# Where the passes of w_in's conversion and the multiplies of h's steps stand in the engines' orders

## The chip, the core and the metric

The kernel runs on one core of a Trainium2 chip. Five queues work at the same time and meet only through semaphores: TensorE (PE in the profile; its weight loads are PEld), VectorE (DVE), ScalarE (ACT), GpSimd (POOL) and the DMA queue of SyncE (SP). Each carries out its own instructions in the order in which the program issues them. The metric is the time of one execution in microseconds (us); lower is better.

## The reference: what is computed

Windowed attention over 4 x 576 tokens with 8 heads, then two feed-forward stages, all in fp32 with tolerances that TensorE's fast fp32 format alone doesn't meet:

```python
scores = scale * np.matmul(q, k.transpose(0, 1, 3, 2))     # window of 64, masked
attn = softmax(scores)                                     # exp(s - max) / (sum + 1e-9)
x = matmul(attn, v)                                        # 2304 x 512
h1 = ((x @ w1) * (x @ w2)) @ w3                            # 512 -> 1024
x2 = h1 @ w_out                                            # 1024 -> 512
h = x2 @ w_in                                              # 512 -> 2048
g = h * (1.0 / (1.0 + np.exp(-h)))
out = g @ w_out2                                           # 2048 -> 512
```

The weights arrive as 64-bit floats. The kernel reads them as pairs of 32-bit words and turns them into fp32 itself.

## The kernel before, in words

**Numbers.** A value that goes into TensorE is split in a high part (a cast on ACT) and a low part (value less high part, on DVE or POOL); a product takes three matmuls, high by high, high by low, low by high.

**Conversion of a weight chunk** of 128 x 512 takes these passes: `scale` (ACT, from the high words), `rest` (ACT, from the low words), `fraction` (a shift on DVE), `sign` (an and-or of two SBUF tensors on DVE, after it an add on POOL). `Chunk` (from line 92) does so for weights that are split at once (`high_part` on ACT at line 145, `low_part` at line 149). `Stored` (line 153) does it for w_in and stores the fp32 words in DRAM (`w_in32`), from where the later stage loads them (`r_load`).

**First part, blocks 0 to 5** (`phase_a`, 384 tokens each). A block has 24 units on PE: 16 units of 12 matmuls for x@w1 and x@w2 (`ab`, line 561; the odd ones end in `a`, the multiply of line 569 on DVE, and p's split: an ACT cast and a POOL subtract, lines 81 and 84), then 8 units of 12 matmuls for x2 (`x`, line 581). Before each unit one half of an attention group is issued (`half`): the even half has the scores on PE, the scores' minima on DVE (line 319), the value matmuls (`o`), the transposes of the group before (`t`, line 352), p-transposed's casts on ACT and its subtracts on DVE (lines 362 to 367), and the exponentials on ACT (line 330). The odd half has the normalising on DVE (a reduce, a reciprocal and the multiply of line 342, whose result `sm` the next transposes read), the sums of the values (lines 394 to 398) and the preparation of a later group's q, k and v (lines 284 to 291). So a group is two units, and a block takes 12 groups. Attention ends in block 4.

**w_in's conversion** runs beside blocks 1 to 4. It has 16 chunks. A list `trickle` holds their pieces in order, and `drop` runs one piece per unit, as the first thing behind the half: two loads first, then for each chunk `scale`, `rest`, `fraction`, `sign`, `store` and the load of the chunk after next. That is one chunk in 6 units, or 3 groups.

**Second part.** In the last seven units of block 5, and then in slots s = 1 to 23 of seven steps k = 0 to 6, h is made in seven products of Strassen's kind per slot (`product`, line 743, six matmuls each) into two PSUM tiles: `hx` for k = 0, 2, 4 and `hy` for k = 1, 3, 5, 6. A product that begins a tile afresh (k = 0, 1, 4, 5) has to wait until the tile's last reader is done. `read` adds the pieces up on DVE (line 638, as all of `add` and `sub`) and has ACT take the sigmoid; `multiply` (DVE) makes g, `divide` splits it (ACT cast, POOL subtract), and `out_tile` multiplies it with w_out2 (line 797, six matmuls, k = 0 to 5). `background` does, in each step, the conversion of w_out2's chunks (`convert_to`, slots 1 to 7), the preparation of the next slot's w_in pieces (`jit_part`, tables `JIT_AT` and, in block 5, `J5`) and of the next x operand (slots 5 to 8). The order in a step is product, read, background, multiply, divide, out_tile.

Of the kernel before, what the change touches and what calls it, by code (L numbers as in the profile page):

```python
# [42 lines left out]
def tile_window_attention_ffn(ctx, tc, qkv, vp, mask, ident, w1, w2, w3t, w_out, w_in, w_out2, out):  # L43
# [109 lines left out]
    class Stored(Chunk):  # L153
# [3 lines left out]
        def pieces(self):  # L157
# [16 lines left out]
            def sign():  # L174
                nc.vector.scalar_tensor_tensor(
                    out=self.b, in0=self.high, scalar=-0x80000000, in1=self.b, op0=ALU.bitwise_and, op1=ALU.bitwise_or
                )
                nc.gpsimd.tensor_tensor(out=self.b, in0=self.b, in1=self.r, op=ALU.add)
# [4 lines left out]
            return [self.load, scale, rest, fraction, sign, store]  # L183

    weights = {}
    line = []
    done = {"load": 0, "step": 0}
# [214 lines left out]
    def half(h):  # L402
# [4 lines left out]
        if not odd:  # L407
            if g < NG:
                scores(g)
            if 2 <= g <= NG + 1:  # L410
                sums.append(values(g - 2))
                if plain(g - 2):
                    sums.pop()()
# [129 lines left out]
    def phase_a(blk, hooks):  # L543
# [9 lines left out]
        for s in range(16):  # L553
# [11 lines left out]
            if m == 0:  # L565
                a_sb = slot(f"a{blk}_{f}", "st", [2, NB], bufs=4)
                nc.scalar.copy(out=a_sb[:, 0], in_=acc)
            else:
                nc.vector.tensor_tensor(out=a_sb[:, 1], in0=acc, in1=a_sb[:, 0], op=ALU.mult)
                split(p[f][:, 0], p[f][:, 1], a_sb[:, 1], "act", "pool")  # L570
        for o in range(4):
            acc = accumulator(f"x2_{blk}_{o}", [128, NB])
            for f in range(8):
# [6 lines left out]
                for n, (l, r) in enumerate(PASSES):  # L580
# [3 lines left out]
                    )  # L584
            x2 = slot(f"x2s{blk}_{o}", "st", [NB], bufs=4)
# [13 lines left out]
    with tc.manual_schedule():  # L599
# [5 lines left out]
        trickle = []  # L605
        for i in range(16):
# [3 lines left out]
            trickle.append(c.pieces())  # L610
        for a, b in zip(trickle, trickle[2:] + [()] * 2):
            a.extend(b[:1])
        trickle = trickle[0][:1] + trickle[1][:1] + [f for p in trickle for f in p[1:]]

        def drop(n):
            if trickle:
                trickle.pop(0)()

        for blk in range(1, NBLK - 1):
            phase_a(blk, drop)  # L620
        while trickle:
            drop(0)
# [25 lines left out]
        for f in (0, 1, 2, 3, 4, None, None, None, 5, 8, 6, 7, 9, 10, 11, 12, 13, 14, 15):  # L648
# [3 lines left out]
            tag = f"w{f if f < 8 else f + 8}"  # L652
# [30 lines left out]
        def jit_part(s, part):  # L683
# [13 lines left out]
            elif part == 1:  # L697
                sub(nc.vector, a[:, 1], one, f32(a[:, 0]))
                sub(nc.vector, d[:, 1], a22, f32(d[:, 0]))
# [15 lines left out]
        JIT_AT = {0: (2,), 1: (3, 0), 2: (1,), 3: (4,), 4: (5,), 5: (6,)}  # L715
# [46 lines left out]
        def read(s, k):  # L762
# [3 lines left out]
            one, two, three = tmp["v"]  # L766
# [9 lines left out]
            elif k == 4:  # L776
                add(nc.vector, three, x, one)
                finished(s, k, three)
# [80 lines left out]
        def background(s, k):  # L859
# [11 lines left out]
            if 1 <= s < PAIRS and done["step"] < len(line):  # L871
                n = BLOCK_STEPS + 2 * (s - 1) + (k >= 2) + (k >= 5)
                if s < 3:
                    n = BLOCK_STEPS + 3 * (s - 1) + k // 2
                else:
                    n += 2
                convert_to(n)
                loads_to(begin + min(n + 2, 10 if s == 1 else NLINE))
# [9 lines left out]
        def step(s, k):  # L888
            if s < NSLOT:
# [3 lines left out]
                read(s, k)  # L893
            background(s, k)
            multiply()
            divide()
# [7 lines left out]
        J5 = {8: (0, 0), 9: (0, 1), 10: (0, 2), 11: (0, 3), 12: (0, 4), 13: (0, 5), 14: (0, 6)}  # L904
        J5 |= {18: (1, 0), 19: (1, 1), 20: (1, 2), 21: (1, 3), 22: (1, 4), 23: (1, 5)}

        def hooks5(n):
# [14 lines left out]
            if n == 17:  # L922
                t = slot("tmp", "xb", [4, NB])
                tmp["v"] = [t[:, i] for i in range(3)]
                tmp["sg"] = [t[:, 3], xe[:, 2304 - NB : 2304]]
            if n == 16:
                raw[1] = slot("r_w5", "w5", [4, 256])
# [7 lines left out]
            if n >= 8:  # L935
                loads_to(begin + (4 if n < 16 else 5))
            if n in X5:
                X5[n][0](*X5[n][1:])
            if n in J5:
                jit_part(*J5[n])  # L940
# [89 lines left out]
```

## Time and profile before

| | us |
|---|---|
| median of 3 runs | 876.49 (876.15 to 876.94) |
| the profiled execution | 877.07 |
| its span | 875.3 |
| PE busy | 831.3 |
| DVE, ACT, POOL busy | 621.6, 560.8, 533.4 |

The span runs from the first to the last instruction of the program. Busy times are sums over one engine's instructions; matmuls are pipelined, so their busy time is more than what they hold the engine for. The granted clock is full in all slices. A column "idle before" names the engine's pause ahead of an instruction and what ended it.

### The profile page before, as it was taken

How to read it: one execution, taken by the hardware profiler on the slowest of the kernel's cores; microseconds unless marked ns; L12 is line 12 of the kernel's file. 1: busy time of each engine (PE TensorE's matmuls, PEld its weight loads, DVE VectorE, ACT ScalarE, POOL GpSimd, SP SyncE). 2: the span in 40 equal slices, each digit the busy share in tenths (PEclk: the TensorE clock that was granted, in tenths of full speed). 3: DMA queues.
4: the chain of work that ended last, by engine and by line, in shares of the span. 5: the costliest groups of instructions: out<-in, count | busy, mean ns of one | idle time of the engine just before them, and what ended most of it. 6: DMA issues, size and time to landing. Idle time of an engine off the chain costs nothing.

```text
span 875.3 us, 14089 instructions
## 1 busy us (share of the span) xinstructions
PE 831.3 (95%) x4410; PEld 744.7 (85%) x4410; DVE 621.6 (71%) x1404; ACT 560.8 (64%) x1389; POOL 533.4 (61%) x588
## 2 busy tenths in 40 slices
PE   5999999999998998999999999999999999999998
PEld 2455899988998998998999977878889898898896
DVE  5889867688778777877548588878745558655544
ACT  5889778878887788778646465545634345544333
POOL 4768676667666766766656576675644556545341
PEclk9999999999999999999999999999999999999999
DMA  8998234434544544444252451211210300301001
GB/s 289 320 315 275 78 96 128 143 120 148 167 124 128 166 142 126 155 136 132 65 190 91 136 195 49 97 34 39 97 49 25 114 32 25 120 25 34 16 1 72
DMA packets 57130, 102.66 MB, mean 117 GB/s; under 512 B 5472, under 2 KB 34912, under 8 KB 57056
## 3 DMA queue, kind: packets, MB, share of 16 engines
q1 hardware_dynamic: 53600, 97.05, 34.1%
q10 hardware_dynamic: 3456, 4.72, 1.5%
q8 instruction: 35, 0.57, 0.3%
q14 instruction: 39, 0.32, 0.1%
HBM read 88.11 MB, written 13.63 MB: 116 GB/s over the span
## 4 chain that ended last, share of the span: by engine, by line
PE 49%; DVE 17%; ACT 12%; issue 8%; POOL 2%; ACTq 0%; DVEq 0%; POOLq 0%
PE o L797 18%; PE hy L743 9%; PE hx L743 7%; PE ab L561 7%; PE x L581 5%; ACT sm L330 3%; DVE j L638 2%; DVE qkhi L291 1%; DVE sm L342 1%; ACT pt L364 1%; DVE ot L397 1%; DVE sm L319 1%; DVE hl L149 1%; DVE tmp L638 1%; ACT qkhi L284 1%
## 5 line engine op out<-in xcount | busy, mean ns | idle before, releaser
L797 PE MATMUL o<-hl,gp 128*128 128x512 f32 x504 | 133.3, 394 | 0.0
L743 PE MATMUL hy<-xop,j 128*128 128x384 f32 x576 | 116.3, 336 | 4.0 <-DVE tmp L638 4.0
L561 PE MATMUL ab<-xa,hl 128*128 128x384 f32 x576 | 119.0, 341 | 0.0
L561 PE MATMUL ab<-xb,hl 128*128 128x384 f32 x576 | 115.4, 334 | 0.0
L743 PEld LDWEIGHTS hy<-xop,j 128*128 128x128 f32 x576 | 102.5, 188 | 14.2 <-DVE tmp L638 6.4
L797 PEld LDWEIGHTS o<-hl,gp 128*128 128x128 f32 x504 | 93.1, 188 | 13.1
L638 DVE TENSOR_TENSOR tmp<-hy,tmp 128x384 f32<-128x384 f32 x96 | 53.2, 555 | 67.7 <-PE hy L743 38.4
L561 PEld LDWEIGHTS ab<-xb,hl 128*128 128x128 f32 x576 | 101.2, 188 | 0.0
L561 PEld LDWEIGHTS ab<-xa,hl 128*128 128x128 f32 x576 | 99.1, 188 | 0.0
L743 PE MATMUL hx<-xop,j 128*128 128x384 f32 x432 | 87.7, 337 | 4.3 <-DVE tmp L638 3.0
L398 POOL TENSOR_TENSOR xr<-ot 128x128 f32<-128x128 f32 x55 | 33.2, 604 | 93.5 <-DVE ot L397 88.3
L797 PE MATMUL o<-hl,gq 128*128 128x512 f32 x324 | 85.9, 393 | 0.0
L743 PEld LDWEIGHTS hx<-xop,j 128*128 128x128 f32 x432 | 76.0, 188 | 11.3 <-DVE tmp L638 5.2
L288 POOL TENSOR_TENSOR klo<-qk,qkhi 64x192 fp32r<-64x192 f32 x110 | 73.3, 667 | 7.6 <-ACT qkhi L284 2.7
L797 PEld LDWEIGHTS o<-hl,gq 128*128 128x128 f32 x324 | 60.3, 188 | 11.2
L330 ACT ACTIVATE sm<-sm,nm 128x192 f32<-128x192 f32 x144 | 64.5, 450 | 7.0 <-DVE nm L319 5.7
L581 PE MATMUL x<-p,wp 128*128 128x384 f32 x360 | 68.6, 339 | 0.0
L759 ACT ACTIVATE xe<-tmp 128x384 f32<-128x384 f32 x48 | 25.2, 525 | 67.4 <-DVE tmp L638 67.1
L137 POOL TENSOR_TENSOR cv_b<-cv_b,cv_r 128x512 int32<-128x512 int32 x32 | 47.9, 1498 | 25.4 <-DVE cv_b L133 15.7
L581 PEld LDWEIGHTS x<-p,wp 128*128 128x128 f32 x360 | 61.8, 188 | 0.0
L638 DVE TENSOR_TENSOR tmp<-hx,tmp 128x384 f32<-128x384 f32 x48 | 26.7, 555 | 49.1 <-PE hx L743 34.5
L84 POOL TENSOR_TENSOR gp<-tmp,gp 128x384 fp32r<-128x384 f32 x34 | 38.0, 1116 | 35.3 <-ACT gp L81 35.3
(145 smaller groups left out, 1923.9 us busy)
## 6 DMA issues: line engine op xcount, KB each, us to landing
qk<-in_qkv SPq DMA_DIRECT2D x55, 384.0 KB, 3.2
words<-in_w_out SPq DMA_DIRECT2D x24, 512.0 KB, 5.4
r<-w_in SPq DMA_DIRECT2D x22, 512.0 KB, 3.4
words<-in_w3t SPq DMA_DIRECT2D x16, 512.0 KB, 6.0
words<-in_w SPq DMA_DIRECT2D x16, 512.0 KB, 6.5
xe<-in_w_in SPq DMA_DIRECT2D x16, 512.0 KB, 4.5
v<-in_qkv SPq DMA_DIRECT2D x55, 96.0 KB, 2.7
x2d<-x2s ACTq DMA_DIRECT2D x24, 192.0 KB, 1.9
```

The source lines that it names most:

```text
L84: (nc.vector if eng_lo == "dve" else nc.gpsimd).tensor_tensor(out=lo, in0=src, in1=f32(hi), op=ALU.subtract)
L137: nc.gpsimd.tensor_tensor(out=x, in0=b, in1=self.r, op=ALU.add)
L149: eng.tensor_tensor(out=self.parts[:, 1], in0=f32(self.b), in1=f32(self.parts[:, 0]), op=ALU.subtract)
L288: nc.gpsimd.tensor_tensor(out=k_lo[g % 2][hs, h * 192 : h * 192 + 192], in0=t[hs, n], in1=f32(hi[hs, n]), op=ALU.subtract)
L330: nc.scalar.activation(out=x, in_=x, func=AF.Exp, scale=-1.0, bias=nm[:, h : h + 1], accum_out=sums_of[g % 2][:, h, 0:1])
L398: nc.gpsimd.tensor_tensor(out=xr[:, c, r : r + 128], in0=t[:, 0:128], in1=t[:, 128:256], op=ALU.add)
L561: nc.tensor.matmul(acc, lhsT=w[:, l, fs], rhs=x[k // 2][:, k % 2, r, :], start=(k == 0 and n == 0), stop=(k == 3 and n == 2),)
L581: nc.tensor.matmul(acc, lhsT=wp[f][:, l, o * 128 : (o + 1) * 128], rhs=p[f][:, r, :], start=(f == 0 and n == 0), stop=(f == 7 and n == 2),)
L638: eng.tensor_tensor(out=out, in0=a, in1=b, op=op)
L743: nc.tensor.matmul(bank[name], lhsT=w[:, l, at + kt], rhs=x[:, kt, r, :], start=(fresh and kt == 0 and n == 0), stop=(kt == 1 and n == 2), ...
L759: nc.scalar.activation(out=sg, in_=src, func=AF.Sigmoid)
L797: nc.tensor.matmul(oacc[t], lhsT=g[:, l, cols], rhs=weights["out", 2 * p + i][:, r, :], start=(p == 0 and i == 0 and n == 0), stop=(p == P ...
```

## The change

It changes five things.

1. w_in's passes no longer run first in a unit. A dictionary `between` holds them by unit, and `squeeze` runs them at three places: DVE's passes in an even half behind the scores' minima, ahead of p-transposed's subtracts; ACT's passes in an odd unit ahead of p's cast, or ahead of x2's copy.
2. `sign` is cut in two halves of 256 columns, in two even units; the POOL add is issued with the second. A chunk is spread over more units (scale in unit 6i+1, rest 6i+3, fraction 6i+4, the signs 6i+6 and 6i+8, the store 6i+10, the load of chunk i+1 in 6i+2). Signs and store of the last chunk are issued behind block 4.
3. In h's steps the multiply of k = 2 runs ahead of the background, that of k = 6 in the next slot's step 0, ahead of that step's background; those of k = 4 and 5 stay behind it.
4. The sum of k = 4 is written over hx in PSUM, in place of a third temporary; sigmoid and multiply read it there. The two results `sg` lie in one tile, and raw[1] lies in `xr`.
5. w_out2's conversion: chunk 5 moves into block 5, and slots 1 and 2 get fewer passes; the second conversion of a slot stands in k = 3 in place of 5. The subtract of piece d gets a step of its own (part 7), and the casts of part 0 and the subtract of part 1 come one step earlier.

```diff
@@ -171,19 +171,27 @@
-            def sign():
+            def sign(i):
+                n = slice(i * 256, i * 256 + 256)
                 nc.vector.scalar_tensor_tensor(
-                    out=self.b, in0=self.high, scalar=-0x80000000, in1=self.b, op0=ALU.bitwise_and, op1=ALU.bitwise_or
+                    out=self.b[:, n], in0=self.high[:, n], scalar=-0x80000000, in1=self.b[:, n],
+                    op0=ALU.bitwise_and, op1=ALU.bitwise_or,
                 )
-                nc.gpsimd.tensor_tensor(out=self.b, in0=self.b, in1=self.r, op=ALU.add)
+                if i:
+                    nc.gpsimd.tensor_tensor(out=self.b, in0=self.b, in1=self.r, op=ALU.add)
...
-            return [self.load, scale, rest, fraction, sign, store]
+            return [self.load, scale, rest, fraction, lambda: sign(0), lambda: sign(1), store]
...
+    between, unit_of = {}, [0]
+
+    def squeeze(u):
+        if u in between:
+            between.pop(u)()
...
@@ -407,6 +415,7 @@
             if g < NG:
                 scores(g)
+            squeeze(unit_of[0])
...
@@ -567,6 +576,7 @@
                 nc.vector.tensor_tensor(out=a_sb[:, 1], in0=acc, in1=a_sb[:, 0], op=ALU.mult)
+                squeeze(unit_of[0] - 1)
                 split(p[f][:, 0], p[f][:, 1], a_sb[:, 1], "act", "pool")
...
@@ -582,6 +592,7 @@
+            squeeze(unit_of[0] - 1)
             x2 = slot(f"x2s{blk}_{o}", "st", [NB], bufs=4)
...
@@ -602,24 +613,32 @@
-            trickle.append(c.pieces())
-        for a, b in zip(trickle, trickle[2:] + [()] * 2):
-            a.extend(b[:1])
-        trickle = trickle[0][:1] + trickle[1][:1] + [f for p in trickle for f in p[1:]]
+            load, scale, rest, fraction, sign0, sign1, store = c.pieces()
+            at = 6 * i
+            chunks.append((load, store))
+            between[at + 1], between[at + 3] = scale, rest
+            between[at + 4], between[at + 6], between[at + 8] = fraction, sign0, sign1
 
         def drop(n):
-            if trickle:
-                trickle.pop(0)()
-
+            u = unit_of[0]
+            if u % 6 == 2 and 0 < u // 6 < 15:
+                chunks[u // 6 + 1][0]()
+            if u >= 10 and (u - 10) % 6 == 0:
+                chunks[(u - 10) // 6][1]()
+            unit_of[0] += 1
...
@@ -645,11 +664,11 @@
-        for f in (0, 1, 2, 3, 4, None, None, None, 5, 8, 6, 7, 9, 10, 11, 12, 13, 14, 15):
+        for f in (0, 1, 2, 3, 4, 5, None, None, None, 6, 7, 8, 9, 10, 11, 12, 13, 14, 15):
...
-            tag = f"w{f if f < 8 else f + 8}"
+            tag = f"w{f if f < 6 else f + 10 if f < 14 else f - 8}"
...
@@ -696,6 +715,7 @@
                 sub(nc.vector, a[:, 1], one, f32(a[:, 0]))
+            elif part == 7:
                 sub(nc.vector, d[:, 1], a22, f32(d[:, 0]))
...
-        JIT_AT = {0: (2,), 1: (3, 0), 2: (1,), 3: (4,), 4: (5,), 5: (6,)}
+        JIT_AT = {0: (2, 0), 1: (3, 1), 2: (7,), 3: (4,), 4: (5,), 5: (6,)}
...
             elif k == 4:
-                add(nc.vector, three, x, one)
-                finished(s, k, three)
+                add(nc.vector, x, x, one)
+                finished(s, k, x)
...
@@ -869,13 +889,9 @@
-                n = BLOCK_STEPS + 2 * (s - 1) + (k >= 2) + (k >= 5)
-                if s < 3:
-                    n = BLOCK_STEPS + 3 * (s - 1) + k // 2
-                else:
-                    n += 2
+                n = BLOCK_STEPS + 2 * (s - 1) + 1 + (k >= 3) + (s > 1 or k >= 6)
                 convert_to(n)
-                loads_to(begin + min(n + 2, 10 if s == 1 else NLINE))
+                loads_to(begin + min(n + 2, NLINE))
...
@@ -891,9 +907,15 @@
                 product(s, k)
                 read(s, k)
+            if k in (0, 2):
+                multiply()
+            if k == 0:
+                divide()
             background(s, k)
-            multiply()
-            divide()
+            if 2 < k < 6:
+                multiply()
+            if k < 6:
+                divide()
...
-                tmp["v"] = [t[:, i] for i in range(3)]
-                tmp["sg"] = [t[:, 3], xe[:, 2304 - NB : 2304]]
+                tmp["v"] = [t[:, i] for i in range(2)]
+                tmp["sg"] = [t[:, i] for i in (2, 3)]
...
-                raw[1] = slot("r_w5", "w5", [4, 256])
+                raw[1] = slot("r_xr", "xr", [4, 256])
```

DVE in blocks 1 to 4, between two multiplies `a` of line 569 (578 after the change). Names: pt is p-transposed, rs and sm the sums and the weights of attention, ot the sums of the values, cv_b the converted words, xe the raw ones. Before:

```order
L365 TENSOR_TENSOR pt_978<-t_3952,pt_978 128x2x128
L367 TENSOR_TENSOR pt_976<-t_3952,pt_976 64x64 x2
L172 TENSOR_SCALAR cv_b<-cv_b 128x512
L338 TENSOR_REDUCE rs_3945<-es_82 128x2
L340 RECIPROCAL rs_3945<-rs_3945 128x2
L342 TENSOR_TENSOR sm_73<-sm_73,rs_3945 128x384
L396 TENSOR_TENSOR ot_3983<-o_3948,ot_3983 64x256
L397 TENSOR_TENSOR ot_3983<-o_3948,ot_3983 64x256
L291 TENSOR_TENSOR qkhi_3989<-qk_3839,qkhi_3989 64x256
L175 SCALAR_TENSOR_TENSOR cv_b<-xe,cv_b 128x512
L569 TENSOR_TENSOR a_2_3978<-ab_5_4003,a_2_3978 128x384
```

And now:

```order
L327 ISA nm_3951 128x1
L172 TENSOR_SCALAR cv_b<-cv_b 128x512
L373 TENSOR_TENSOR pt_978<-t_3960,pt_978 128x2x128
L375 TENSOR_TENSOR pt_976<-t_3960,pt_976 64x64 x2
L346 TENSOR_REDUCE rs_3952<-es_82 128x2
L348 RECIPROCAL rs_3952<-rs_3952 128x2
L350 TENSOR_TENSOR sm_73<-sm_73,rs_3952 128x384
L404 TENSOR_TENSOR ot_3991<-o_3956,ot_3991 64x256
L405 TENSOR_TENSOR ot_3991<-o_3956,ot_3991 64x256
L299 TENSOR_TENSOR qkhi_3997<-qk_3844,qkhi_3997 64x256
L578 TENSOR_TENSOR a_2_3986<-ab_5_4009,a_2_3986 128x384
```

The fraction stood between the subtracts of pt and the normalising, the sign ahead of the multiply a. The fraction now stands behind the minima (line 327), and each half of the sign stands at that same place in the next two groups (line 176).

POOL in the same blocks; klo, vhl and p are low parts, xr the sums of the values, L178 (181) the add of the conversion. Before:

```order
L398 TENSOR_TENSOR xr<-ot_3983 128x128
L288 TENSOR_TENSOR klo_75<-qk_3839,qkhi_3989 64x192 x2
L84 TENSOR_TENSOR vhl_3994<-v_3761,vhl_3994 128x3x64
L178 TENSOR_TENSOR cv_b<-cv_b,cv_r 128x512
L84 TENSOR_TENSOR p_3780<-a_2_3978,p_3780 128x384
```

And now:

```order
L296 TENSOR_TENSOR klo_75<-qk_3685,qkhi_3836 64x192 x2
L84 TENSOR_TENSOR vhl_3841<-v_3607,vhl_3841 128x3x64
L84 TENSOR_TENSOR p_3785<-a_0_3825,p_3785 128x384
L181 TENSOR_TENSOR cv_b<-cv_b,cv_r 128x512
L406 TENSOR_TENSOR xr<-ot_3911 128x128
```

The add stood ahead of p's subtract; now it stands behind it and ahead of the next sums of values.

DVE in a slot of h's steps that has two conversions (lines 130, 133, 149); hx and hy are the products, j the next slot's weights, tmp and xe the sums and g. Before, from k = 1 to k = 4:

```order
L638 TENSOR_TENSOR tmp<-hy_1_6635,tmp 128x384
L130 TENSOR_SCALAR cv_b<-cv_b 128x512
L133 SCALAR_TENSOR_TENSOR cv_b<-words,cv_b 128x512
L149 TENSOR_TENSOR hl<-cv_b,hl 128x512
L638 TENSOR_TENSOR j_0_6002<-r_6178,j_0_6002 128x512
L638 TENSOR_TENSOR j_3_6005<-r_6178,j_3_6005 128x256
L638 TENSOR_TENSOR tmp<-hx_0_6618,tmp 128x384
L638 TENSOR_TENSOR tmp<-hy_1_6635,tmp 128x384
L638 TENSOR_TENSOR tmp<-hx_4_6697,tmp 128x384
```

And now:

```order
L657 TENSOR_TENSOR tmp<-hy_1_6654,tmp 128x384
L657 TENSOR_TENSOR j_0_6020<-r_6204,j_0_6020 128x512
L657 TENSOR_TENSOR tmp<-hx_0_6620,tmp 128x384
L657 TENSOR_TENSOR j_3_6023<-r_6204,j_3_6023 128x256
L657 TENSOR_TENSOR tmp<-hy_1_6654,tmp 128x384
L130 TENSOR_SCALAR cv_b<-cv_b 128x512
L133 SCALAR_TENSOR_TENSOR cv_b<-words,cv_b 128x512
L149 TENSOR_TENSOR hl<-cv_b,hl 128x512
L657 TENSOR_TENSOR hx_4_6714<-hx_4_6714,tmp 128x384
```

The multiply of k = 2 (tmp<-hx_0) had five subtracts and passes ahead of it behind the sum of k = 1, now one; the conversion comes behind the sum of k = 3.

## Rows read from the trace of the kernel before

**Rows 1.** The waits of PE, longest in total: us, times, longest.

```profile
PE t L352 <- DVE sm L342: 17.8, 20, 1.7
```

**Rows 2.** The chain in order of time, end of block 0: start, length, what.

```profile
139.50 4.17 PE x L581 x24
...
160.51 4.17 PE ab L561 x24
```

**Rows 3.** Windows, blocks 1 to 3, then 4: length; busy PE, PEld, DVE, ACT, POOL.

```profile
160.27:368.08 207.81, 193.35 (x1191) 189.18 (x1190) 163.39 (x515) 168.48 (x493) 140.35 (x192) 1.00 0.47 145
368.08:434.29 66.21, 61.96 (x381) 60.91 (x380) 49.63 (x153) 51.05 (x149) 43.42 (x58) 1.00 0.33 106
```

**Rows 4.** Windows: slots 1 to 7 of h's steps together, then slot 8.

```profile
492.54:613.52 120.98, 112.83 (x547) 97.34 (x547) 99.21 (x132) 65.13 (x129) 78.97 (x69) 1.00 0.27 93
613.52:629.16 15.64, 15.64 (x79) 14.05 (x79) 13.17 (x17) 11.05 (x22) 9.73 (x9) 1.00 0.23 85
```

**Rows 5.** Timeline, two groups of block 2: start, us, engine, line, what, idle before.

```profile
243.67 0.90 DVE L172 TENSOR_SCALAR cv_b<-cv_b 128x512 int32<-128x512 int32 x1
...
245.58 0.52 PE L352 MATMUL t<-id_sb,sm 128*128 128x128 f32 x3 [0.72 <-DVE sm L342]
...
246.68 0.84 DVE L175 SCALAR_TENSOR_TENSOR cv_b<-xe,cv_b 128x512 int32<-128x512 int32 x1
...
249.29 1.30 POOL L178 TENSOR_TENSOR cv_b<-cv_b,cv_r 128x512 int32<-128x512 int32 x1
...
249.30 0.42 DVE L365 TENSOR_TENSOR pt<-t,pt 128x256 fp32r<-128x256 f32 x1 [0.64 <-ACT pt L364]
...
250.54 1.00 POOL L84 TENSOR_TENSOR p<-a,p 128x384 fp32r<-128x384 f32 x1
...
250.71 1.25 DVE L342 TENSOR_TENSOR sm<-sm,rs 128x384 f32<-128x384 f32 x1
...
252.10 0.52 PE L352 MATMUL t<-id_sb,sm 128*128 128x128 f32 x3 [1.08 <-DVE sm L342]
```

**Rows 6.** Timeline, one group of block 0, where no conversion of w_in runs.

```profile
133.78 0.56 DVE L569 TENSOR_TENSOR a<-ab,a 128x384 f32<-128x384 f32 x1
...
134.37 0.51 ACT L81 CAST q<-a 128x384 fp32r<-128x384 f32 x1 [0.83 <-DVE a L569]
...
136.93 0.56 DVE L342 TENSOR_TENSOR sm<-sm,rs 128x384 f32<-128x384 f32 x1
...
139.01 0.49 PE L352 MATMUL t<-id_sb,sm 128*128 128x128 f32 x3
139.12 0.56 DVE L569 TENSOR_TENSOR a<-ab,a 128x384 f32<-128x384 f32 x1
```

**Rows 7.** Groups of instructions by line: ACT's scale; busy us, mean ns | idle before.

```profile
L164 ACT ACTIVATE cv_b<-xe 128x512 f32<-128x512 f32 x16 | 10.4, 652 | 0.0
```

**Rows 8.** Timeline, slot 4 and the start of slot 5.

```profile
554.42 0.79 PE L743 MATMUL hx<-xop,j 128*128 128x384 f32 x3 [0.66 <-DVE tmp L638]
...
560.28 1.67 POOL L137 TENSOR_TENSOR cv_b<-cv_b,cv_r 128x512 int32<-128x512 int32 x1 [1.09 <-DVE cv_b L133]
...
560.72 1.78 DVE L638 TENSOR_TENSOR j<-sums,j 128x512 fp32r<-128x512 f32 x1
...
563.49 1.31 PE L743 MATMUL hy<-xop,j 128*128 128x384 f32 x6 [0.46 <-DVE tmp L638]
564.09 0.94 DVE L638 TENSOR_TENSOR xe<-tmp,xe 128x384 f32<-128x384 f32 x1 [0.65 <-ACT xe L759]
```

**Rows 9.** Instructions on the tile tmp: count, then min/median/max ns.

```profile
L638 DVE TENSOR_TENSOR tmp<-hx,tmp x48: 543/558/559, 477.7 to 858.5; 128x384 f32<-128x384 f32 x48
...
L638 DVE TENSOR_TENSOR xe<-tmp,xe x48: 544/558/1659, 484.5 to 864.6; 128x384 f32<-128x384 f32 x48
```

**Rows 10.** Timeline, block 2, among its units of x2.

```profile
285.20 1.30 POOL L178 TENSOR_TENSOR cv_b<-cv_b,cv_r 128x512 int32<-128x512 int32 x1
...
285.27 1.64 DVE L342 TENSOR_TENSOR sm<-sm,rs 128x384 f32<-128x384 f32 x1
```

More of the change, by code (lines that the diff above doesn't have):

```diff
@@ L604, in tile_window_attention_ffn @@
         phase_a(0, lambda n: steps_to(W12_B + 24 + (n + 1) * (20 - W12_B) // 6, (nc.vector, nc.gpsimd)))
-        trickle = []
+        chunks = []
         for i in range(16):
@@ L609, in tile_window_attention_ffn @@
             c = Stored(None, w_in[k * 128 : (k + 1) * 128, cols], xe[:, i % 2 * 1024 : i % 2 * 1024 + 1024], w_in32[k, :, cols])
-            trickle.append(c.pieces())
-        for a, b in zip(trickle, trickle[2:] + [()] * 2):
-            a.extend(b[:1])
-        trickle = trickle[0][:1] + trickle[1][:1] + [f for p in trickle for f in p[1:]]
-        def drop(n):
-            if trickle:
-                trickle.pop(0)()
+            load, scale, rest, fraction, sign0, sign1, store = c.pieces()
[3 more added lines that the diff above has]
+            between[at + 4], between[at + 6], between[at + 8] = fraction, sign0, sign1
+        def drop(n):
+            u = unit_of[0]
[4 more added lines that the diff above has]
+            unit_of[0] += 1
+        chunks[0][0]()
+        chunks[1][0]()
         for blk in range(1, NBLK - 1):
             phase_a(blk, drop)
-        while trickle:
-            drop(0)
+        for u in sorted(between):
+            between.pop(u)()
+        chunks[15][1]()
         late.close()
@@ L762, in read @@
         def read(s, k):
-            one, two, three = tmp["v"]
+            one, two = tmp["v"]
             x, y = bank["hx"], bank.get("hy")
@@ L903, in tile_window_attention_ffn @@
         X5 |= {10: (x_sum, 3), 11: (x_op, 0, 3), 13: (x_op, 0, 4), 14: (x_op, 0, 5), 16: (x_op, 0, 6)}
-        J5 = {8: (0, 0), 9: (0, 1), 10: (0, 2), 11: (0, 3), 12: (0, 4), 13: (0, 5), 14: (0, 6)}
-        J5 |= {18: (1, 0), 19: (1, 1), 20: (1, 2), 21: (1, 3), 22: (1, 4), 23: (1, 5)}
+        J5 = {8: (0, 0), 9: (0, 1), 10: (0, 7, 2), 11: (0, 3), 12: (0, 4), 13: (0, 5), 14: (0, 6)}
+        J5 |= {18: (1, 0), 19: (1, 1), 20: (1, 7, 2), 21: (1, 3), 22: (1, 4), 23: (1, 5)}
         def hooks5(n):
@@ L935, in hooks5 @@
             if n >= 8:
-                loads_to(begin + (4 if n < 16 else 5))
+                loads_to(begin + (4 if n < 16 else 6))
             if n in X5:
@@ L939, in hooks5 @@
             if n in J5:
-                jit_part(*J5[n])
+                for part in J5[n][1:]:
+                    jit_part(J5[n][0], part)
         phase_a(NBLK - 1, hooks5)
```

## The prediction

> **What bounds the kernel now.** PE is busy for 831 of the span's 875, so it sets the end wherever it doesn't wait, and the question is where it waits and for whom. I read the waits of PE first: the largest is that of the transposes `t` for `sm`, the normalised weights from DVE [rows 1]. Then each stretch is set against what PE needs there. In block 0, with no conversion of w_in beside it, the chain of waits is all PE, and four groups take 160.51 - 139.50 = 21.01, or 5.25 a group, 4.17 of it the 24 matmuls [rows 2]. Twelve such groups are 63.0. Blocks 1 to 3 take 207.81, that is 69.3 each [rows 3]. In the second part a slot without conversion takes 15.64, all of it PE; slots 1 to 7 take 120.98, that is 17.3 each [rows 4]. So two stretches hold what can be won:
>
> - blocks 1 to 3: 207.81 - 3 x 63.0 = 18.7; block 4: 66.21 less 63.0, and about 1.1 more because its last groups lack scores or transposes (estimate: half of the 2 x 1.08 that two groups hold beyond their matmuls), so 4.3. Together 23.0.
> - slots 1 to 7: 120.98 - 7 x 15.64 = 11.5.
>
> **Why blocks 1 to 4 wait.** The timeline of two groups shows two stalls [rows 5]. The fraction stands ahead of the normalising and takes 0.90; the transposes wait 0.72. Then the sign takes 0.84 ahead of the multiply a, and POOL's add takes 1.30 ahead of p's subtract, which so runs from 250.54 to 251.54, into the normalising multiply: that one takes 1.25, against 0.56 in block 0 [rows 6], and the transposes wait 1.08. The multiply ends 0.42 behind POOL's subtract, so it stood still while POOL ran. This comes back every 3 groups, once per chunk.
>
> The Trainium skill (SBUF — State Buffer, section Who interferes with whom) has a rule for it: VectorE and GpSimd share a port pair, held as an exclusive lock for a whole instruction by whoever starts first, and a VectorE instruction with two SBUF inputs takes part. The 1.25 agrees. The rule speaks against cutting the sign in two, which takes the lock once more per chunk: if each of the 16 second halves cost one more stall like the shorter of the two, 0.72, it would be 11.5 and the time 860.
>
> **Edits 1 and 2, part by part.** DVE's passes move into a pause: behind the minima DVE waits 0.64 for ACT's casts of pt [rows 5]. A half sign has 256 columns. It lies between 0.37 (256 of 384 columns of the undisturbed two-input multiply's 0.56 [rows 6]) and 0.84, the whole sign [rows 5]. I take 0.4, as the undisturbed row is of the same kind, and a little more where POOL is in the middle of a low part. The pause covers 0.64, and what runs over moves pt's subtracts, not the exponentials that the normalising waits for. So the fractions, the halves and the sixteen extra instructions cost nothing; without that cover each would delay `sm` by its own length.
>
> ACT's scale, 0.65 [rows 7], now stands ahead of p's cast, where ACT idles 0.83 for the multiply a [rows 6]; `rest`, a pass of the same size, stands there too. Both fit: nothing. Among x2's units they come ahead of x2's copy, which no matmul of the same unit waits for.
>
> The POOL add now stands behind p's subtract and ahead of `xr`, which waits for DVE. It can start when that subtract ends, about when the normalising multiply is due. If the multiply is already waiting, I expect it to go first, as in rows 5, where it ran right behind p's subtract; then only the next subtract on q comes some 0.2 late. The other order is a rival below.
>
> On SP loads and stores keep their number. The load of chunk i+1 now waits for a sign of the same unit, and the q, k, v loads behind it come up to 2 late; they are issued about two groups (10.5) before their use: nothing. The last chunk's signs and store move behind block 4, ahead of a load that is first used eight units later: nothing.
>
> What is late next is the loop of DVE and ACT. From one multiply a to the next, block 0 takes 139.12 - 133.78 = 5.34, over PE's 5.25, and the slack of `sm` is 139.01 - 136.93 - 0.56 = 1.5 [rows 6]. Eight such groups lose 0.7, and the adds' 0.2 to 0.3 come on top two or three times, so the slack is about used up at the end of the 16 `ab` units. I leave 0.5 per block for it, 2.0 in all (between 0 and 5). Edits 1 and 2: 23.0 - 2.0 = **21.0 less**.
>
> **Edits 3 to 5, part by part.** Two waits come back in slots 1 to 7 [rows 8]: hx for k = 4, 0.66, for k = 2's multiply, which is queued behind the background; and hy for k = 1, 0.46, for the sum of k = 6, which is behind a conversion in k = 5 and a piece's subtract of 1.78 that met POOL's 1.67. The multiply of k = 2 now goes first: two steps of 15.64 / 7 = 2.2 less the product's 1.3 give it 3.1, and it needs some 1.2 with its sigmoid. The conversion leaves k = 5, so the sum of k = 6 comes about a step earlier. Both waits go.
>
> What comes in their place is DVE's load. It is busy 99.21 / 7 = 14.2 per slot [rows 4], waits for POOL included, and pauses twice for about 0.65 while a multiply at the head of its queue waits for a sigmoid [rows 8]. That is 15.5 of 15.64: no room. The conversion in k = 3 now delays the sums of k = 4 and 5, and the product of k = 6 adds onto the tile that k = 5's sum must have read. I expect it to wait 0.85 in slots 3 to 5 (two full conversions, as before), 0.5 in slot 6, 1.0 in slot 7, where the x operands' subtracts stand, and 0.1 to 0.2 in slots 1 and 2, which lose passes: 4.3 in all, between 0 (the pauses overlap with others) and 11.5 (nothing won). So 11.5 - 4.3 = **7.2 less**.
>
> The sum over hx in place: reads of hx take 0.56 at most in all 48 cases, the multiplies with two SBUF operands up to 1.66 [rows 9], so k = 4's multiply can gain up to 1.1. What writing the sum to PSUM costs no row shows; between nothing and the 0.56 of one more such instruction per slot, all of it on DVE, and I take nothing, since the sum writes as many columns as before. Chunk 5's passes fall in block 5, where PE doesn't wait. The last multiply lies beside the last output tiles either way.
>
> **Sum.** 21.0 + 7.2 = 28.2. From the profiled execution's 877.07 that gives 848.9; the median of the runs is 0.6 lower, so 848.3.
>
> **Rivals.**
>
> - *All stalls go.* The slack holds and DVE fits in: 23.0 + 11.5, so 876.5 - 34.5 = 842. Against: the 15.5 of 15.64. Chance 0.13.
> - *The add takes the port first.* If p's subtract ends just ahead of the normalising, the add starts and the multiply waits for all of it: 1.64 in place of 0.56 is on record [rows 10]. That is 1.08, of which I set 0.8 beyond what slack is left, for each of 16 chunks: 12.8 back, so 861. For: the add is ready long before, so it starts at once. Against: p's subtract is itself pushed a little by the half sign ahead of it, so the multiply is usually waiting already. Chance 0.15.
> - *The second part wins nothing.* DVE and POOL, not the order, hold a slot at 17.3: 21.0 alone, 855.5. Chance 0.13.
> - *Slower.* hx is now read until k = 4's multiply, and the next slot's k = 0 begins hx afresh. If that multiply came too late, PE would wait in all 23 slots, also in those that have no wait today. Between the two products lie three steps less a product, about 5.4; the sum, the piece's subtract (up to 1.78) and the multiply with its sigmoid need 3 to 3.5. It decides from 28.2 / 23 = 1.2 per slot, with DVE over 3 behind; at 1.6 per slot the time is 885. Against: slot 8 runs at 15.64 with DVE busy 13.17 [rows 4]. Chance 0.03.
>
> That the order is not as written is no rival: each engine runs its instructions in program order.
>
> **How the numbers follow.** My forecast has the remaining 0.56. A change of 0.2% (1.8 us) is about what a measurement of this kernel can tell from none. Only the last rival and a stack of shortfalls in both parts (0.03 within 0.2%) don't end faster: faster 0.94, same 0.03, slower 0.03. The range goes from 841, all stalls gone, to 861, which takes in each single shortfall but not both together.
>
> **What would show it.** Right: blocks 1 to 3 at 63 to 64.5, the wait of `t` for `sm` nearly gone, the normalising multiply near 0.56, fraction and half signs inside DVE's pause; slots 3 to 5 at 16 to 17 with hy waiting for a DVE sum at k = 6, and hx no longer waiting at k = 4. Wrong: blocks at 66 with normalising multiplies over 1 (the add's port), slots still at 17.3, or hx waiting at k = 0 in slots 9 to 23.

## The result, and the profile after

The changed kernel takes 847.83 us (median of 4 runs, 847.28 to 849.21); the kernel before took 876.72 beside it (876.15 to 876.97). The ratio is 0.9674, with a 95% interval from 0.9657 to 0.969. The profiled execution took 847.28, its span 845.5, at full granted clock. So 28.9 us are gone where 28.2 were forecast. The windows show that the sum came out so close by two errors of opposite sign.

Waits of PE in the changed kernel (us, times, longest), against [rows 1]:

```profile
PE t L360 <- DVE sm L350: 3.6, 5, 1.1
PE x L591 <- POOL q L84: 1.3, 4, 0.4
...
PE hy L763 <- DVE tmp L657: 0.5, 1, 0.5
```

And before, for the products of h's steps:

```profile
PE hy L743 <- DVE tmp L638: 4.0, 5, 1.4
PE hx L743 <- DVE tmp L638: 3.0, 5, 0.9
```

The wait of the transposes fell from 17.8 to 3.6; one of the five that are left is in block 1, none in blocks 2 to 4. The waits for hx are no longer in the list. The stretches, in windows of the changed kernel (length; busy PE, PEld, DVE, ACT, POOL; granted clock), are blocks 1, 2, 3 and 4, then slots 1 to 7:

```profile
159.65:226.07 66.42, 64.54 (x400) 63.19 (x398) 52.34 (x174) 56.05 (x165) 45.25 (x64) 1.00 0.49 154
226.07:289.98 63.91, 63.49 (x399) 62.99 (x398) 53.59 (x176) 56.36 (x165) 47.25 (x65) 1.00 0.50 155
289.98:353.87 63.89, 63.49 (x400) 62.99 (x398) 53.63 (x176) 56.36 (x165) 47.23 (x65) 1.00 0.50 155
...
353.87:415.34 61.47, 61.15 (x381) 60.83 (x380) 49.31 (x158) 51.33 (x149) 43.08 (x58) 1.00 0.37 115
473.58:584.20 110.62, 110.14 (x547) 98.07 (x547) 96.28 (x129) 63.40 (x125) 78.91 (x67) 1.00 0.24 85
```

Against [rows 3] blocks 1 to 3 gave 207.81 - 194.22 = 13.6 and block 4 gave 66.21 - 61.47 = 4.7; against [rows 4] slots 1 to 7 gave 120.98 - 110.62 = 10.4. Slot 15, which took 16.11 before, is at 15.64. That is 29.2 of the spans' 29.8; the other 0.6 lies ahead of block 0, where both programs are the same. The first part thus gave 18.3 where the prediction has 21.0, the second 10.8 where it has 7.2.

Blocks 2 and 3 run as forecast. The timeline of a group in block 2 of the changed kernel shows how:

```profile
248.86 0.78 DVE L176 SCALAR_TENSOR_TENSOR cv_b<-xe,cv_b 128x256 int32<-128x256 int32 x1
...
250.07 1.01 POOL L84 TENSOR_TENSOR p<-a,p 128x384 fp32r<-128x384 f32 x1
...
250.60 0.16 DVE L346 TENSOR_REDUCE rs<-es 128x2 f32<-128x4 f32 x1 [0.22 <-ACT sm L338]
...
250.99 0.56 DVE L350 TENSOR_TENSOR sm<-sm,rs 128x384 f32<-128x384 f32 x1
251.04 1.66 POOL L181 TENSOR_TENSOR cv_b<-cv_b,cv_r 128x512 int32<-128x512 int32 x1
...
252.07 0.49 PE L360 MATMUL t<-id_sb,sm 128*128 128x128 f32 x3
```

The half sign lies in DVE's pause; DVE still waits 0.22 for the exponentials. The multiply takes 0.56 (1.25 in [rows 5]), and it is now the add that stands still: 1.66 against 1.30. The transposes wait for nobody.

Block 1 is the exception:

```profile
167.99 0.66 ACT L164 ACTIVATE cv_b<-xe 128x512 f32<-128x512 f32 x1 [3.07 <-DMA xe<-in_w_in]
...
170.26 0.47 PE L394 MATMUL o<-pt,vhl 128*128 128x256 f32 x2 [0.55 <-POOL p L84]
...
171.79 0.52 PE L360 MATMUL t<-id_sb,sm 128*128 128x128 f32 x3 [0.82 <-DVE sm L350]
```

The first scale now stands in the block's second unit. Its load was issued at 162.96, behind the q, k, v loads, and landed 5.0 later. ACT waits 3.07 for it, and behind ACT's queue p, the exponentials and the transposes are late. The kernel before had the scale a unit later, at 168.40, and ACT didn't wait.

In slots 1 to 7 what is left stands in slots 4, 5 (0.2 each) and 7 (0.74). Slot 4 of the changed kernel, as a window and around its second conversion:

```profile
520.50:536.34 15.84, 15.84 (x80) 13.98 (x80) 14.34 (x20) 9.58 (x20) 12.06 (x10) 1.00 0.36 133
```

```profile
521.24 0.94 DVE L657 TENSOR_TENSOR tmp<-tmp 128x384 f32<-128x384 f32 x1 [0.65 <-ACT tmp L779]
...
528.00 0.56 DVE L657 TENSOR_TENSOR tmp<-hy,tmp 128x384 f32<-128x384 f32 x1 [0.73 <-PE hy L763]
...
529.96 1.50 DVE L149 TENSOR_TENSOR hl<-cv_b,hl 128x512 fp32r<-128x512 f32 x1
...
533.55 0.54 DVE L657 TENSOR_TENSOR tmp<-hy,tmp 128x384 f32<-128x384 f32 x1
...
534.15 0.99 PEld L763 LDWEIGHTS hy<-xop,j 128*128 128x128 f32 x6 [0.36 <-DVE tmp L657]
```

The product of k = 6 (the last row is its weight load) waits for the sum of k = 5, the wait that was forecast, at a quarter of its size: the slot is 0.2 over 15.64, in place of 0.85.

### The profile page after: what moved, and what is told of

Same layout as the page of the kernel before. It is cut to its first block, busy times and chain, and to the rows that moved or that the text cites. A ratio compares the mean times of both kernels' runs of the same rounds, so it can differ in the third digit from the quotient of the medians.

```text
span 845.5 us, 14148 instructions
## 1 busy us (share of the span) xinstructions
PE 825.3 (98%) x4410; PEld 744.5 (88%) x4410; DVE 611.0 (72%) x1420; ACT 560.7 (66%) x1389; POOL 532.2 (63%) x588
## 4 chain that ended last, share of the span: by engine, by line
PE 59%; POOL 12%; ACT 7%; issue 6%; DVE 3%; DMA 1%; ACTq 0%; POOLq 0%; SPq 0%; DVEq 0%
PE o L817 22%; PE hy L763 11%; PE ab L570 9%; PE hx L763 9%; PE x L591 5%; POOL klo L296 4%; POOL vhl L84 2%; POOL xr L406 2%; POOL p L84 2%; ACT sm L338 2%; POOL q L84 1%; ACT qkhi L292 1%; POOL cv_b L181 1%; PE t L360 1%; ACT ot L403 1%
## 5 line engine op out<-in xcount | busy, mean ns | idle before, releaser
L84 POOL TENSOR_TENSOR gp<-tmp,gp 128x384 fp32r<-128x384 f32 x56 | 63.6, 1136 | 79.4 <-ACT gp L81 77.8
L779 ACT ACTIVATE tmp<-hx 128x384 f32<-128x384 f32 x48 | 23.6, 492 | 113.3 <-DVE hx L657 69.2
L84 POOL TENSOR_TENSOR gq<-tmp,gq 128x384 fp32r<-128x384 f32 x36 | 40.0, 1112 | 72.6 <-ACT gq L81 72.6
L296 POOL TENSOR_TENSOR klo<-qk,qkhi 64x192 fp32r<-64x192 f32 x110 | 68.1, 619 | 7.6 <-ACT qkhi L292 2.7
```

The costliest lines, as they stand in the source:

```text
L84: (nc.vector if eng_lo == "dve" else nc.gpsimd).tensor_tensor(out=lo, in0=src, in1=f32(hi), op=ALU.subtract)
L296: nc.gpsimd.tensor_tensor(out=k_lo[g % 2][hs, h * 192 : h * 192 + 192], in0=t[hs, n], in1=f32(hi[hs, n]), op=ALU.subtract)
L779: nc.scalar.activation(out=sg, in_=src, func=AF.Sigmoid)
```

## The experiments

Each time is the median of 4 or 5 runs; in brackets stands the ratio to the kernel before, run on the same chip, with its 95% interval. The diffs are against the changed kernel. The theory behind the first four: the two parts are independent, block 1 waits for its load, and the add's place decides whether the normalising meets POOL.

**1. The first part alone** (edits 1 and 2 made, 3 to 5 not).

```diff
-            if k in (0, 2):
-                multiply()
...
-        JIT_AT = {0: (2, 0), 1: (3, 1), 2: (7,), 3: (4,), 4: (5,), 5: (6,)}
+        JIT_AT = {0: (2,), 1: (3, 0), 2: (1,), 3: (4,), 4: (5,), 5: (6,)}
```

> Edits 1 and 2 alone: w_in's passes at their new places and the sign in two halves; the second part stays as before. The prediction on record has 21.0 less than before for this half of the change, so 855.7. Read from the stretches of the changed kernel's trace it is less: blocks 1 to 3 went from 207.81 to 194.22 and block 4 from 66.21 to 61.47, together 18.3, so 858.4, with block 1 at 66.4 and blocks 2 and 3 at 63.9 each. If the two halves of the change act on each other, block lengths differ from those of the changed kernel, or the slots from those of before (17.3).

Measured: 858.39 (0.979, 0.9777 to 0.9803). Its blocks 1 to 4 take 255.86, the changed kernel's 255.69; its slots 1 to 7 take 121.01, as before. So 18.0 less, not 21.0.

**2. The second part alone** (edits 3 to 5 made, 1 and 2 not).

```diff
-            squeeze(unit_of[0])
...
+            trickle.append(c.pieces())
```

> Edits 3 to 5 alone: order of the multiplies, the sum in place, the new places of w_out2's passes; blocks 1 to 4 stay as before. The prediction on record has 7.2 less than before for this half, so 869.5. Read from the changed kernel's slots (120.98 to 110.62, and slot 15 from 16.11 to 15.64) it is 10.8 less, so 865.9. If the slots gained because blocks 1 to 4 hand over in a better state, less than 10.8 is found here.

Measured: 865.28 (0.9871, 0.9857 to 0.9884). Slots 1 to 7 take 110.73, blocks as before. 18.0 + 11.1 = 29.1 against 28.9 for both: the parts are independent, and each was mis-sized by itself.

**3. Block 1's load.**

```diff
+            if n in (16, 18):
+                chunks[n // 2 - 8][0]()
...
-        chunks[0][0]()
-        chunks[1][0]()
```

> The changed kernel, with the loads of w_in's first two chunks issued in units 16 and 18 of block 0 in place of behind it. In the changed kernel ACT waits 3.07 for the first of these loads, ahead of the scale that now stands in block 1's second unit, and block 1 takes 66.42 against 63.9 of blocks 2 and 3. Theory: that load is all of it, so block 1 falls to 64.0 and the time to 847.8 - 2.4 = 845.4. Rival: the first group of attention in block 1 is late for another reason (the block's first operands), so block 1 stays at 66.4 and the time at 847.8.

Measured: 844.19 (0.9632, 0.9619 to 0.9645), below the changed kernel's interval. Block 1 and its first scale, which waits for nothing:

```profile
159.49:223.09 63.60, 63.50 (x399) 63.00 (x398) 52.30 (x174) 56.05 (x165) 45.18 (x64) 1.00 0.45 144
```

```profile
164.66 0.67 ACT L164 ACTIVATE cv_b<-xe 128x512 f32<-128x512 f32 x1
```

The load was all of block 1's excess. The gain of the medians, 3.6, is more than the 2.8 that block 1 shows between the two profiled executions; the section on the hardware has a likely reason.

**4. The add ahead of p's subtract.**

```diff
-                if i:
-                    nc.gpsimd.tensor_tensor(out=self.b, in0=self.b, in1=self.r, op=ALU.add)
...
+            if u >= 9 and (u - 9) % 6 == 0:
+                chunks[(u - 9) // 6][2]()
```

> The changed kernel, with POOL's add of w_in's conversion back in the unit after, ahead of p's subtract; DVE's and ACT's passes stay at their new places. Theory: the place of the add decides whether the normalising multiply meets a running POOL instruction. Then it takes 1.2 to 1.3 again once per chunk in place of 0.56, the transposes wait up to 1.08 for it, and up to 16 x 0.8 = 13 comes back: 856 to 861. Rival: the place of DVE's passes took away the waits and the add may stand anywhere: multiplies at 0.56 and 847.8 to 849.

Measured: 853.74 (0.9739, 0.9726 to 0.9752). 5.9 came back, less than expected, and by another way. In block 2 of this kernel, one chunk's add (it began at 257.58), then the start of x2:

```profile
258.50 0.79 DVE L351 TENSOR_TENSOR sm<-sm,rs 128x384 f32<-128x384 f32 x1
258.83 1.33 POOL L84 TENSOR_TENSOR p<-a,p 128x384 fp32r<-128x384 f32 x1
...
273.56 1.28 POOL L182 TENSOR_TENSOR cv_b<-cv_b,cv_r 128x512 int32<-128x512 int32 x1
274.80 1.32 POOL L84 TENSOR_TENSOR q<-a,q 128x384 fp32r<-128x384 f32 x1
...
276.18 0.62 PE L592 MATMUL x<-q,wp 128*128 128x384 f32 x2 [1.55 <-DVE ot L406]
```

The multiply takes 0.79, not 1.25, and the transposes don't wait for it. What waits is x2: the add stands ahead of q's last subtract in POOL's queue, and its operand is late by 1.6 once per block. (The row names DVE; that sum had long been done, and the subtract ends at 276.12.) The theory fell: an add ahead of p's subtract doesn't by itself bring back the long multiply. The multiply comes in 0.33 ahead of p's subtract here, and that subtract then waits; in [rows 5] it came in 0.17 behind the subtract's start.

But this is not quite the old place of the add. Counted from 0, it stands in units 3, 9, 15 and 21 of a block here, in units 5, 11, 17 and 23 in the kernel before. There, in block 2, it was ahead of q's first subtract, and x2 waited 0.60 for the last one:

```profile
267.25 1.29 POOL L178 TENSOR_TENSOR cv_b<-cv_b,cv_r 128x512 int32<-128x512 int32 x1
268.50 1.00 POOL L84 TENSOR_TENSOR q<-a,q 128x384 fp32r<-128x384 f32 x1
...
280.25 0.63 PE L581 MATMUL x<-q,wp 128*128 128x384 f32 x2 [0.60 <-POOL q L84]
```

So most of the 5.9 is the price of unit 15, which ends in x2's last operand, and what the old place cost isn't measured. All waits of x2 for it, against 1.3 in the changed kernel:

```profile
PE x L592 <- DVE ot L406: 6.6, 4, 1.9
```

**5. The sign in one piece.**

```diff
-                n = slice(i * 256, i * 256 + 256)
+                n = slice(0, 512)
...
-            between[at + 4], between[at + 6], between[at + 8] = fraction, sign0, sign1
+            between[at + 4], between[at + 8] = fraction, sign1
```

> The changed kernel with the sign in one piece of 512 columns, at the place of its second half. Measured in the changed kernel: a half takes 0.78 beside POOL's low part where the whole took 0.84 at its old place, the pause behind the minima is 0.64, and DVE waits another 0.22 for the exponentials behind pt's subtracts. Theory: the whole sign takes 1.1 to 1.2 there, which is 0.2 to 0.35 more than both pauses, once per chunk: 16 x 0.2 to 0.35 = 3 to 5.5, of which the slack in x's units takes a third, so 849.5 to 851.5. Rival 1, the one that speaks against the cut: each half takes the port once more, so the whole sign is better: 846 to 847. Rival 2: the late subtracts of pt hold the value matmuls up, over 853.

Measured: 847.13 (0.9666, 0.9652 to 0.9681), no difference; blocks 2 and 3 take 64.05 and 64.01. The whole sign takes 1.04 there, 0.4 over the pause, and the theory's loss did not come. The first rival's 847 can't be told from the changed kernel by the runs, but blocks 2 and 3 are no shorter than its 63.91 and 63.89. No worth of edit 2's cut shows, either way.

**6. DVE's passes behind pt's subtracts.** A first form also issued the load of later words ahead of the sign that reads the buffer, so that the second half of each chunk's sign waited for that load and took the wrong words (931.1); it says nothing about the places. The second form:

```diff
-            between[at + 4], between[at + 6], between[at + 8] = fraction, sign0, sign1
+            behind[at + 4], behind[at + 6], behind[at + 8] = fraction, sign0, sign1
...
+            if u in behind:
+                behind.pop(u)()
```

> The changed kernel, with DVE's passes of w_in (fraction and both halves) issued behind pt's subtracts, ahead of the normalising, in the same units and ahead of the loads and stores of their unit; ACT's passes and the add stay. The first half of the change gave 18.0, of which the add's place was worth 5.9. Theory: the rest, 12.1, is the place of DVE's passes, so about 860: a pass of 0.43 to 0.8 less the 0.22 that DVE waits there lies ahead of the normalising in each group. Rival: what counts is that the sign left the place ahead of the multiply a; with the passes ahead of the normalising the slack of the weights takes most of it: 848 to 852.

Measured: 864.53 (0.9866, 0.9851 to 0.9881). That is 16.7 more than the changed kernel, where the whole first part had won 18.0. For the fraction this is the old place; the halves of the sign never stood here (the whole one stood ahead of the multiply a). Block 2 of this kernel:

```profile
255.13 0.88 DVE L176 SCALAR_TENSOR_TENSOR cv_b<-xe,cv_b 128x256 int32<-128x256 int32 x1
...
256.09 1.28 POOL L181 TENSOR_TENSOR cv_b<-cv_b,cv_r 128x512 int32<-128x512 int32 x1 [0.36 <-DVE rs L346]
...
256.32 1.47 DVE L350 TENSOR_TENSOR sm<-sm,rs 128x384 f32<-128x384 f32 x1
...
257.93 0.52 PE L360 MATMUL t<-id_sb,sm 128*128 128x128 f32 x3 [1.05 <-DVE sm L350]
```

Here the second half ends at 256.01, the add starts at 256.09, 0.23 ahead of the multiply, and the multiply ends 0.42 behind the add. This is the rival in which the add goes first; what brings it about is a late DVE, whose second half lets the add go just ahead of the multiply. The Trainium skill (SBUF — State Buffer, section Who interferes with whom) says that issue order decides who blocks. These rows and those of the changed kernel agree: 1.47 for the multiply in the one order, 1.66 for the add in the other. Experiments 4 and 6 give back 22.6 together where 18.0 were won: neither puts the old order back, so each is the price of its own places and not a share of the gain.

**7. The multiplies in their old order.**

```diff
-            if k in (0, 2):
-                multiply()
-            if k == 0:
-                divide()
             background(s, k)
...
+            multiply()
+            divide()
```

> The changed kernel with edit 3 undone: every multiply of h's steps behind the background of its step, that of k = 6 in its own step. Theory: the order ended hx's wait for k = 4 (4.3 in slots 1 to 7 of the kernel before, by the waits of PE), so 0.4 to 0.6 per slot comes back: 850.5 to 852. Rival: the conversions, now in k = 0 and 3, leave k = 2's background with one subtract alone, so k = 2's multiply is early either way: 847.8 to 848.5.

Measured: 847.23 (0.9666, 0.965 to 0.9682), slots 1 to 7 at 110.94: nothing, as the rival has it.

**8. The sum in a third temporary.**

```diff
-                add(nc.vector, x, x, one)
-                finished(s, k, x)
+                add(nc.vector, three, x, one)
+                finished(s, k, three)
```

> The changed kernel with edit 4 undone: the sum of k = 4 goes into a third temporary in SBUF and the multiply reads it there. Theory: the sum over hx in PSUM costs 0.567 against 0.558, nothing, and spares the multiply of k = 4 the POOL instruction beside it; undone, that multiply takes up to 1.6 in place of 0.55 where POOL is busy. DVE is short by 0.2 per slot in slots 4, 5 and 7 already, so 0.3 to 0.8 in slots 2 to 7 comes back: 849.5 to 852.5. Rival: DVE has slack at that point: 847.8 to 848.5.

Measured: 848.39 (0.9684, 0.967 to 0.9698); by the runs this can't be told from the changed kernel. In the profiled execution, at 849.71 the slowest of its four, slots 1 to 7 take 112.85, 2.2 more, mostly in slot 5:

```profile
549.17 2.28 POOL L657 TENSOR_TENSOR t<-xra 128x768 f32<-128x768 f32 x1
549.69 2.18 DVE L657 TENSOR_TENSOR xe<-tmp,xe 128x384 f32<-128x384 f32 x1
...
552.39 0.79 PE L763 MATMUL hy<-xop,j 128*128 128x384 f32 x3 [1.58 <-DVE tmp L657]
```

The mechanism is there, a multiply of 2.18 beside POOL, but its worth stays open between nothing and 2.

**9. The conversions in k = 2 and 5.**

```diff
-                n = BLOCK_STEPS + 2 * (s - 1) + 1 + (k >= 3) + (s > 1 or k >= 6)
+                n = BLOCK_STEPS + 2 * (s - 1) + 1 + (k >= 2) + (k >= 5)
```

> The changed kernel, with the two conversions of a slot back in k = 2 and k = 5 in place of 0 and 3; the multiplies keep their new places. Undoing the multiplies' order alone moved slots 1 to 7 from 110.62 to 110.94, nothing. Theory: it is the conversions that decide, each has to lie where no sum behind it is needed at once. In k = 5 it lies ahead of the sum of k = 6 again, so hy waits for k = 1 (0.46 and more per slot, 4.0 in all before): 3 to 5 more, 851 to 853. Rival: either of the two edits suffices alone, so this one moves nothing too: 847.3 to 848.5.

Measured: 853.51 (0.9738, 0.9725 to 0.9752), slots 1 to 7 at 116.46, 5.8 more. At the start of its slot 5:

```profile
538.22 1.78 DVE L657 TENSOR_TENSOR j<-sums,j 128x512 fp32r<-128x512 f32 x1
...
540.40 0.55 DVE L657 TENSOR_TENSOR tmp<-hy,tmp 128x384 f32<-128x384 f32 x1
...
541.00 1.31 PE L763 MATMUL hy<-xop,j 128*128 128x384 f32 x6 [1.13 <-DVE tmp L657]
```

The old wait is back: hy for k = 1 waits for the sum of k = 6, queued behind the conversion and the 1.78.

**10. The conversions and the order of the multiplies both as before.**

```diff
-                n = BLOCK_STEPS + 2 * (s - 1) + 1 + (k >= 3) + (s > 1 or k >= 6)
+                n = BLOCK_STEPS + 2 * (s - 1) + 1 + (k >= 2) + (k >= 5)
...
-            if k in (0, 2):
-                multiply()
```

> The changed kernel, with the conversions back in k = 2 and 5 and every multiply behind the background of its step, as before; the sum in place and chunk 5's passes in block 5 stay. Theory: with the conversion of k = 2 ahead of the multiply of k = 2, hx's wait for k = 4 (0.66) joins hy's for k = 1: 7 to 10 more than the changed kernel, 855 to 858, near the 858.4 of the first half alone. Rival: the sum in place and the three passes fewer carry most of the slots' gain: 848 to 852.

Measured: 855.12 (0.9757, 0.9743 to 0.977), slots 1 to 7 at 117.75. Its waits of PE:

```profile
PE hx L763 <- DVE tmp L657: 2.6, 4, 0.7
PE hy L763 <- DVE tmp L657: 2.1, 3, 1.3
```

The order of the multiplies counts only where a conversion stands ahead of k = 2's: then hx's wait returns. Of the slots' 10.4, the conversions' places hold 5.8 and both together 7.1. The other 121.01 - 117.75 = 3.3 belong to the rest: the sum in place, three passes fewer, the subtracts of the pieces. These weren't taken apart further.

**11. A version with two more moves** on top of experiment 3.

```diff
+        while held:
+            held.pop()()
...
-            (7, 4): lambda j: x_sum(3), (7, 5): lambda j: x_op(j, 3),
+            (7, 6): lambda j: x_sum(3), (8, 0): lambda j: x_op(j, 3),
```

> The changed kernel with the two early loads (844.2) and two further moves. In blocks 1 to 4, in the 16th unit, v's split and the loads of v are issued behind the split of q, so POOL's subtract on q no longer stands behind v's low part (0.66), for which x<-q waits 0.44 in blocks 2 to 4. In slots 7 and 15 the last sum of the x operands moves from k = 4 to k = 6, and the operands 3 and 4 one to two steps back, out of the queue ahead of the sum that hy waits 0.65 for. Theory: both waits go, 3 x 0.44 + 0.65 = 2.0 less, 842.2. Rival: blocks are held by the loop of DVE and ACT (5.33 a group), which only shows at x<-q, so they stay at 63.9 and the slots alone gain: 843.5.

Measured: 844.73 (0.9641, 0.9628 to 0.9654); one of its five executions took 2121.6, for a reason that no trace shows. It can't be told from experiment 3's 844.19. The slots gained 0.7, as expected; the blocks gained nothing, as the rival has it. In the blocks x2 no longer waits for q, but the last transposes of a block now wait for ACT's cast of the next block's operand:

```profile
286.43 0.52 PE L360 MATMUL t<-id_sb,sm 128*128 128x128 f32 x3 [0.70 <-ACT xb L81]
```

Blocks 2 and 3 take 64.2. So the fastest kernel measured is that of experiment 3, with 3.6 less than the changed one.

## Why the prediction was right, and where it was not

- **The total** is right by luck: the first part won 2.7 less than forecast (18.3 against 21.0), the second 3.6 more (10.8 against 7.2). The mechanisms are judged one by one below.
- **What bounds the kernel** held: the gain lies in the two stretches that were named, and in neither is more than the ceilings of 23.0 and 11.5 gone.
- **DVE's pieces in the pause**: right. In blocks 2 to 4 the transposes wait for nobody, also in experiment 4, whose add stands ahead of p's subtract; with the pieces behind pt's subtracts the waits are back (experiment 6). But "I take 0.4" for a half sign was mis-sized: 0.78 measured. The halves run over the pause by 0.14, and this moved pt's subtracts, not the normalising, as the text has it. The whole sign runs over by 0.4 and costs nothing either.
- **"Both fit: nothing"**, on ACT's passes, is the step that failed. It looked at ACT's idle time of a steady group and not at the first scale, whose words must have landed: 2.5 in block 1 (66.42 against 63.9), and 3.6 by the medians of experiment 3. Moving a step earlier moves it toward its load; SP's queue was looked at for the loads behind, not for the first one. Whether ACT's new places gain anything was not tried apart.
- **The add behind p's subtract**: right that the multiply goes first, at 0.56, and the add takes 1.66. What the move is worth stays open: with the add ahead of p's subtract again, in other units, the multiply takes no more than 0.79 (experiment 4), and the late operand of x2 there is the price of a place that the kernel before didn't use.
- **The residual of 0.5 a block**: 0.9 in blocks 2 and 3, -0.4 in block 4 against the estimated floor. The loop of DVE and ACT that the text blames is there. In block 2 of the changed kernel PE's first eight groups take 42.02 (the block begins at 226.07, x2's first matmul at 268.09), or 5.25 each, while DVE's multiplies come every 5.34, and the first wait stands where the text has it, at the end of the 16 `ab` units, at x2's last operand:

```profile
237.17 0.56 DVE L578 TENSOR_TENSOR a<-ab,a 128x384 f32<-128x384 f32 x1
...
242.51 0.56 DVE L578 TENSOR_TENSOR a<-ab,a 128x384 f32<-128x384 f32 x1
...
272.46 0.61 PE L591 MATMUL x<-q,wp 128*128 128x384 f32 x2 [0.30 <-POOL q L84]
```

Eight such groups lose about 0.7 against PE. When experiment 11 took this wait away, another came up at the block's last transposes, and the blocks stayed. That fits a loop that is too long; no run shortened it, so that it makes up the 0.9 is not shown.
- **"4.3 in all"** for slots 1 to 7 was mis-sized: 110.62 - 7 x 15.64 = 1.1 measured. The place was right (hy at k = 6). Slots 3 to 5, forecast at 16 to 17, take 15.64 and twice 15.84; no row stood behind the 0.85. In slot 4 DVE is busy for 14.34 and pauses for 0.73 and 0.65, which all but fills the slot, and PE loses 0.2. That fits a price of what DVE is over 15.64 and not of how late one sum is; no run tests it.
- **The two old waits** went, as forecast. For hy it was the conversion that left k = 5, as the text has it (experiment 9). For hx the text names the multiply alone, but either edit is enough: there is no wait for hx with the old order of the multiplies (experiment 7), none with the old places of the conversions (experiment 9), and 2.6 with both (experiment 10).
- **The sum in PSUM for nothing**: right, its median is 0.567 where the sum in SBUF took 0.558 [rows 9]. What it gains stays open (experiment 8).
- **The rule against the cut**, which the prediction draws from the Trainium skill (SBUF — State Buffer, section Who interferes with whom), at 11.5 for sixteen second halves: the halves do wait beside POOL, 0.35 each, but in the pause, and PE lost nothing.

## What to carry to other kernels

A pass is free in an engine's pause as long as what runs over moves something that nobody waits for; read the pause and the next instruction's releaser, not only the busy share. When a step is moved earlier, follow its first instance to the load that feeds it: a steady group doesn't show it. If an engine is nearly full, ask what a new wait puts it over the period; here that came nearer than how far the order puts one result back. And an experiment that undoes a move has to put the piece back in its old place in the period too, or it prices another place.

## What the runs showed of the hardware

The fraction reads one SBUF operand, and it too stands still beside POOL; here it is with the half sign in the changed kernel, and the whole sign of experiment 5 (count, then min/median/max ns):

```profile
L176 DVE SCALAR_TENSOR_TENSOR cv_b<-xe,cv_b x32: 425/778/826, 179.6 to 414.0; 128x256 int32<-128x256 int32 x32
...
L172 DVE TENSOR_SCALAR cv_b<-cv_b x16: 428/780/791, 174.3 to 409.5; 128x512 int32<-128x512 int32 x16
```

```profile
L176 DVE SCALAR_TENSOR_TENSOR cv_b<-xe,cv_b x16: 692/1044/1056, 184.6 to 413.9; 128x512 int32<-128x512 int32 x16
```

The median of all three is 0.35 over the shortest, which began while POOL stood idle (at 405.62 and 409.51 in the changed kernel). So beside POOL half the columns don't halve such a pass: two halves take 1.56, one whole 1.04.

The load of block 1 lands at different times. In the profiled execution of experiment 7, which took 850.58 where its other three took 846.7 to 847.4, ACT waited 4.87 for it, and the granted clock fell to its lower level, 1.2 GHz, behind PE's pause:

```profile
169.00:172.00 3.00, 0.84 (x6) 0.58 (x4) 0.39 (x2) 2.04 (x7) 0.95 (x1) 1.00 0.47 179
172.00:176.00 4.00, 3.00 (x12) 2.80 (x13) 3.27 (x13) 3.69 (x11) 1.16 (x3) 0.61 0.00 0
176.00:180.00 4.00, 4.00 (x15) 4.00 (x15) 2.78 (x12) 3.34 (x12) 2.24 (x4) 0.53 0.39 123
```

Block 1 took 69.5 there. In experiment 4 the same follows x2's wait in block 1 (granted clock 0.51 from 211.2 to 214.7), which is part of its 5.9. That such executions also make up the changed kernel's spread (one of its four took 849.21, at a mean clock of 0.996) is likely, but wasn't traced.
